# Score products tied to the queue place of the feed-forward products, and a new split of the feed-forward fill, in a fused attention, FFN and MoE kernel

## The chip, the core and the metric

The kernel runs on one core of one Trainium2 chip. The time is device microseconds from the start to the end of one execution. A profile is one execution recorded by the hardware profiler.

## What is computed

Three layers run in one launch. Attention has 4 batches, 8 heads, 576 tokens and 64 channels per head, and each query keeps only the keys whose score reaches its 32nd largest. The second layer is a dense feed-forward network (FFN) from 512 to 2048 and back, with a squared ReLU. The third is a mixture of 8 experts, of which each token uses two.

```python
scores = scale * np.matmul(q, k.transpose(0, 1, 3, 2))
kth = np.partition(scores, -top_k, axis=-1)[..., -top_k:-top_k + 1]
attn = softmax(np.where(scores >= kth, scores, -1e9))
x = attn @ v                                  # 2304 tokens x 512
h = np.maximum(x @ w_in, 0.0)
x = h * h @ w_out
# top 2 of 8 noisy gate logits, then the two experts' outputs, weighted
out[mask] += top2_w[mask, k, None] * (np.maximum(x[mask] @ w1[e], 0.0) @ w2[e])
```

## The kernel before

**Units.** Attention is cut into 80 units. A full unit is two heads of one batch and 128 queries. It has two score tiles of 128 x 576, one per head. A left unit holds the 64 last queries of two heads in one score tile. A unit goes through these steps:

- `scores` (L429) multiplies queries and keys on TensorE (L439: four products for a full unit's tile, eight for a left unit's) into the PSUM tile `ps`. There is one `ps` buffer (L389). ScalarE copies it into the row buffer `sb` (L442, or L444 and L445 for a left unit). A unit has one row buffer, and there are four of them, so a unit takes over the buffer of the unit four before it.
- VectorE searches the 32 largest (L453, L457 and `threshold`, L478). The last steps for one tile are put between the search steps of the next tile.
- `softmax` masks and exponentiates with ScalarE L510, GpSimd L511 and ScalarE L512, one of each per tile.
- TensorE transposes the weights of each tile, four blocks at a time (`transpose4`, L523), and then the last 64 keys and the sums (`rest`, L550 and L551). This last step is the last reader of the row buffer.
- `times_v` (L564) multiplies with V in 20 products. The last of them is noted in `gates`.

**FFN.** When all units of a group of token tiles are done, the FFN of that group, a chunk, is put into a background list. There are seven chunks, of 2, 2, 2, 3, 3, 3 and 3 token tiles. `ffn` (L301) is a generator. Each piece it gives out is one group of three TensorE products: L357 to L359 into PSUM tile `pf` (first matrix) or L320 to L322 into `acc` (second matrix). ScalarE L364, L369, L370 and GpSimd L371 stand between the two. Weights come from HBM on the SP queue (L344, L345), two buffers each. The first two chunks have other forms (`plain`, `divide`).

**Order.** The program is written as one loop over units (L861). In iteration i it puts out, in this order: fills 0 and 1, the first transposition of unit i-1, fill 2, the first score tile of unit i+2, fill 3, the second transposition of unit i-1, fill 4, the second score tile of unit i+2, fill 5, `rest` of unit i-1, fill 6, `times_v` of unit i-1, fill 7. A fill puts out a share of the unit's FFN work, given by the list `FILLS`; what is put out too much or too little is carried over. The unit's FFN work (`rate`) is set so that a chunk's FFN ends about when the next chunk's units do.

The queue order of each engine is not the program's: a planner takes, by its own estimate of times, the ready instruction with the best priority. FFN work has a priority 350 instructions later than its place (`FILL_LATER`, L734), and the copies L442 one that is 300 earlier (`SOON`). `tc.issue_after(x)` keeps instructions behind x in the queue of x's own engine, with no semaphore. All FFN products stand in `with behind()`, which puts them behind the last product of the `times_v` put out last:

```python
def behind():
    return tc.issue_after(gates[-1].ins) if gates else nullcontext()
```

Score products have no such tie before the change. After the 80 units, the FFN of the last chunk and the experts (L640 to L715) run.

Of the kernel before, what the change touches and what calls it, by code (L numbers as in the profile page):

```python
# [17 lines left out]
P = 128  # L18
# [10 lines left out]
IN_PSUM = 14  # L29
LEFT_WEIGHT = 0.6  # L30
FILLS = [0.02, 0.1, 0.15, 0.2, 0.15, 0.1, 0.2, 0.1]
ROUTE_WAIT = 30
LAST_WAIT = 8
EXPERT_WAIT = 60
EARLY = 3
SOON = 300
FILL_LATER = 350
PROMPT = 350
CONVERT_LATER = 200
# [15 lines left out]
def attention_ffn_moe(ctx: ExitStack, tc: tile.TileContext, q, k, v, w_ffn, w_route, noise, w_exp, out,  # L55
# [3 lines left out]
    nc = tc.nc  # L59
# [5 lines left out]
    NF = DFF // P  # L65
    NFE = F // P
    NC = DM // P
    HS = S // 2
    NFULL = S // P
    LEFT = S - NFULL * P  # L70
# [10 lines left out]
    whole = [nc.dram_tensor(f"whole{tag}{f}", (P, 2, DM), F32, kind="Internal").ap() for f in range(NF)]  # L81
# [105 lines left out]
    def route(t0, xrs):  # L187
# [50 lines left out]
        nc.gpsimd.tensor_tensor(mb[:, 0:nt, :], o1, o2, op=ALU.add)  # L238
        yield LAST_WAIT if after else ROUTE_WAIT
        pp = ps_f.tile([P, DM], F32, name="pf")  # L240
# [49 lines left out]

    vpools = []

    gates = []

    def behind():
        return tc.issue_after(gates[-1].ins) if gates else nullcontext()
# [4 lines left out]
    def ffn(t0, nt, xT):  # L301
        n = nt * P
        acc = []
        plain, divide = t0 == 0, t0 == CHUNKS[0]

        def second(f, wo, gt):
            if f == 0:
                while fronts:
                    front()
                acc.extend(ps_acc.tile([P, DM], F32, name="acc") for _ in range(nt))  # L310
            for tt in range(nt):
                sl = slice(tt * P, (tt + 1) * P)
                if plain:
                    with behind():
                        nc.tensor.matmul(acc[tt], gt[:, 0, sl].bitcast(F32), wo[:, 0, :].bitcast(F32),
                                         start=(f == 0), stop=(f == NF - 1))
                    yield True, 0.8
                    continue
                with behind():
                    nc.tensor.matmul(acc[tt], gt[:, 0, sl], wo[:, 0, :], start=(f == 0), stop=False)  # L320
                    nc.tensor.matmul(acc[tt], gt[:, 0, sl], wo[:, 1, :], start=False, stop=False)  # L321
                    nc.tensor.matmul(acc[tt], gt[:, 1, sl], wo[:, 0, :], start=False, stop=(f == NF - 1))  # L322
                yield True, 0.65

        prev = None
        for f in range(NF):
            if after:
                wi, wo = (mpools[0].tile([P, 2, DM], F32R, name=name, bufs=3) for name in ("wif", "wof"))
            else:
                wi, wo = (fpool.tile([P, 2, DM], F32R, name=name, bufs=2) for name in ("wi", "wo"))  # L330
            if plain:
                for i, w in enumerate((wi, wo)):
                    nc.sync.dma_start(w[:, 0, :].bitcast(F32), whole[f][:, i])
            elif divide:
                raw = vpools[0].tile([P, 2 * DM], U32, name="raw", bufs=4 if keep is not None else 2).bitcast(F32)
                nc.sync.dma_start(raw, whole[f].rearrange("p a d -> p (a d)"))
                for i, (w, eng) in enumerate(((wi, nc.gpsimd), (wo, nc.vector))):
                    part = raw[:, i * DM:(i + 1) * DM]
                    with prompt():
                        nc.scalar.activation(w[:, 0, :], part, AF.Copy)  # L340
                        eng.tensor_tensor(w[:, 1, :], part, w[:, 0, :].bitcast(F32), op=ALU.subtract)
                    nc.sync.dma_start(wsc[f][:, i], w.bitcast(F32))
            else:
                nc.sync.dma_start(wi.bitcast(F32), wsc[f][:, 0])  # L344
                nc.sync.dma_start(wo.bitcast(F32), wsc[f][:, 1])  # L345
            ph = after[0].tile([P, DM], F32, name="ph") if after else ps_f.tile([P, DM], F32, name="pf")
            for c in range(NC):
                sl = slice(c * P, (c + 1) * P)
                if plain:
                    with behind():  # L350
                        nc.tensor.matmul(ph[:, 0:n], wi[:, 0, sl].bitcast(F32), xT[:, 0, c, 0:n].bitcast(F32),
                                         start=(c == 0), stop=(c == NC - 1))
                    if c < NC - 1:
                        yield False, 0.2 * nt
                    continue
                with behind():
                    nc.tensor.matmul(ph[:, 0:n], wi[:, 0, sl], xT[:, 0, c, 0:n], start=(c == 0), stop=False)  # L357
                    nc.tensor.matmul(ph[:, 0:n], wi[:, 0, sl], xT[:, 1, c, 0:n], start=False, stop=False)  # L358
                    nc.tensor.matmul(ph[:, 0:n], wi[:, 1, sl], xT[:, 0, c, 0:n], start=False, stop=(c == NC - 1))  # L359
                if c < NC - 1:  # L360
                    yield False, 0.163 * nt
            r = fpool.tile([P, CH], F32, name="r")
            with prompt():
                nc.scalar.activation(r[:, 0:n], ph[:, 0:n], AF.Relu)  # L364
                gt = fpool.tile([P, 2, CH], F32R, name="gt")
                if plain:
                    nc.scalar.activation(gt[:, 0, 0:n].bitcast(F32), r[:, 0:n], AF.Square)
                else:
                    nc.scalar.activation(r[:, 0:n], r[:, 0:n], AF.Square)  # L369
                    nc.scalar.activation(gt[:, 0, 0:n], r[:, 0:n], AF.Copy)  # L370
                    nc.gpsimd.tensor_tensor(gt[:, 1, 0:n], r[:, 0:n], gt[:, 0, 0:n].bitcast(F32), op=ALU.subtract)  # L371
            yield True, 0.163 * nt
            if prev is not None:
                yield from second(*prev)
            prev = (f, wo, gt)
        yield True, 0.65
        yield from second(*prev)
        if t0 + nt == NTT:
            for e in range(EARLY):
                nc.vector.tensor_scalar(base[:, e:e + 1], base[:, e:e + 1], float(e * NT + PARTS[0][1]), None,  # L380
                                        op0=ALU.max)
        routing.append([route(t0, evacuate(acc)), 1])
        if not after:
            fronts.append(t0)
# [44 lines left out]
    def scores(pairs, sb, whole, then):  # L429


        ps = ps_s.tile([P, 2, 512], F32, name="ps")
        for i, (st, kt, par) in enumerate(pairs):
            for n in range(2):
                if whole:
                    at, w = n * HS, HS
                else:
                    at, w = ((LEFT * par, NFULL * P), (0 if par else NFULL * P, LEFT))[n]
                nc.tensor.matmul(ps[:, n, 0:w], st, kt[:, at:at + w], start=(i == 0), stop=(i == len(pairs) - 1))  # L439
        with tc.high_priority(SOON):  # L440
            if whole:
                nc.scalar.activation(sb.rearrange("p (n s) -> p n s", n=2), ps[:, :, 0:HS], AF.Copy)  # L442
# [3 lines left out]
        w = apool.tile([P, S], F32, name="w", bufs=4)  # L446
        if keep is not None:
# [3 lines left out]
            for i in range(SEGS + 1):  # L451
# [3 lines left out]
                if i > 0:  # L455
                    sl, top = parts[i - 1]
# [58 lines left out]
    def recip(sm):  # L515
        with tc.high_priority(SOON):
            nc.scalar.add(sm, sm, EPS)
# [10 lines left out]
    def finish(av, rt, dst, j, off, n, plain):  # L528
        if plain:
            with tc.high_priority(SOON):  # L530
                nc.vector.tensor_tensor(dst[:, 0, j, off:off + n].bitcast(F32), av[:, 0:n], rt, op=ALU.mult)
            return
        x = apool.tile([P, P], F32, name="x", bufs=4)
        with tc.high_priority(SOON):
            if n == P:
# [189 lines left out]
    state = {"safe": True, "due": 0.0, "chunk": 0, "routed": 0}  # L725
# [4 lines left out]
    def step(n):  # L730

        state["due"] += n
        at = tc.cur_priority
        tc.cur_priority = at + FILL_LATER  # L734
        while state["due"] > 0 and (background or routing):
# [125 lines left out]
    for i in range(NU):  # L861
        credit = rate(i)

        def fill(part):
            step(credit * part)

        fill(FILLS[0] + FILLS[1])
        for f, a in todo.get(i, []):
            f(*a)
        q_split(i + AHEAD + 2)  # L870
        if i + AHEAD < NU:
            start(i + AHEAD)
        else:
            flush()
        if i > 0:
            next(gens[i - 1])
        fill(FILLS[2])
        if i + AHEAD < NU:
            next(gens[i + AHEAD])
        fill(FILLS[3])  # L880
        if i > 0:
            next(gens[i - 1])
        fill(FILLS[4])
        if i + AHEAD < NU:
            next(gens[i + AHEAD])
        fill(FILLS[5])
        if i > 0:
            next(gens[i - 1])
        fill(FILLS[6])
        if i > 0:  # L890
            close(i - 1)
        fill(FILLS[7])
        side(convs, CONVERTS, CONVERT_LATER)
        if i >= ZEROS_FROM:
            side(zeros, 1, ZEROS_LATER)
# [232 lines left out]
```

## Time and profile before

| what | before |
|---|---|
| median of 3 runs | 1333.97 us (1333.89 to 1338.11) |
| the profiled execution's own time | 1336.86 us |
| its span, first to last instruction | 1335.1 us |
| PE, matmul busy | 1241.5 us (93%) |
| PEld, weight loads busy | 1071.8 us (80%) |
| DVE / ACT / POOL busy | 899.2 / 856.6 / 746.2 us |
| mean granted TensorE clock | 0.985 of full speed |

PE is TensorE's matmuls, PEld its weight loads, which overlap them. DVE is VectorE, ACT ScalarE, POOL GpSimd, SP the engine whose queue starts most transfers. Matmuls are pipelined, and the duration shown of one is longer than the distance to the next, so a busy PE need not be a PE at its peak. Idle time of an engine matters only where that engine sets the end.

### The profile page before, as it was taken

The numbers are of one execution on the slowest core, as the hardware profiler recorded it, in microseconds if no ns is written. First come the engines' busy times: TensorE is split into PE (matmuls) and PEld (weight loads), VectorE is DVE, ScalarE is ACT, GpSimd is POOL, SyncE is SP. The second block draws the span as 40 slices with busy tenths as digits, with TensorE's granted clock in tenths as the row PEclk, the third lists the DMA queues.
The fourth block names the chain that finished last, engine by engine and source line by source line (L and its number), as shares of the span: only waits on it lengthen the run. The fifth ranks groups of instructions, "written<-read, shape, count | busy, mean of one in ns | idle before, by whom it ended". The sixth has DMA issues, their size and how long they took to land.

```text
span 1335.1 us, 26136 instructions
## 1 busy us (share of the span) xinstructions
PE 1241.5 (93%) x8030; PEld 1071.8 (80%) x8030; DVE 899.2 (67%) x4557; ACT 856.6 (64%) x1886; POOL 746.2 (56%) x1243
## 2 busy tenths in 40 slices
PE   3769889989998999999999999999999999999997
PEld 2556667777887888888888888899899999988886
DVE  8999989998986899978677410255534343444554
ACT  6878879989897889987878653543433333332443
POOL 5857798887786676767655635333432241503221
PEclk9889999999999999999999999999999999999999
DMA  9998886875675554366534689366643443534464
GB/s 333 361 368 292 274 273 235 309 260 181 219 231 193 166 174 157 106 211 204 168 115 158 205 297 332 113 198 197 192 151 117 143 136 119 174 103 143 141 202 140
DMA packets 93302, 270.06 MB, mean 202 GB/s; under 512 B 11612, under 2 KB 11740, under 8 KB 93152
## 3 DMA queue, kind: packets, MB, share of 16 engines
q1 hardware_dynamic: 83872, 239.91, 54.3%
q0 software_dynamic: 9280, 28.40, 5.9%
q8 instruction: 65, 1.06, 0.3%
q14 instruction: 85, 0.70, 0.2%
HBM read 209.90 MB, written 60.45 MB: 202 GB/s over the span
## 4 chain that ended last, share of the span: by engine, by line
PE 61%; ACT 13%; DVE 11%; DMA 7%; issue 5%; POOL 3%; SPq 0%; POOLq 0%; DVEq 0%; ACTq 0%
PE pa L564 5%; PE ph L693 5%; PE ph L695 4%; PE ph L694 4%; PE acc L676 4%; PE acc L674 4%; PE acc L675 4%; PE ps L439 4%; PE pa L523 3%; PE acc L322 3%; PE acc L320 3%; PE acc L321 3%; DMA raww<-in_exp 3%; PE pf L357 2%; PE pf L358 2%
## 5 line engine op out<-in xcount | busy, mean ns | idle before, releaser
L511 POOL TENSOR_TENSOR sb<-sb,w 128x576 f32<-128x576 f32 x144 | 205.8, 1430 | 63.3 <-ACT w L510 59.3
L453 DVE MAX8 m<-sb 128x8 f32<-128x115 f32 (+1 forms) x720 | 190.3, 264 | 53.1 <-ACT sb L442 47.6
L457 DVE MATCH_REPLACE8 w<-m,sb 128x115 f32<-128x115 f32 (+1 forms) x720 | 187.1, 263 | 0.0
L699 ACT ACTIVATE ht<-ph 128x384 fp32r<-128x384 f32 (+1 forms) x128 | 55.8, 436 | 195.2 <-PE ph L695 177.0
L715 POOL DMA_INDIRECT out<-y,info x40 | 45.1, 1127 | 242.4 <-DVE y L714 224.7
L439 PE MATMUL ps<-K,qt 128*128 128x288 f32 (+2 forms) x640 | 131.4, 333 | 43.9 <-ACT sb L442 30.0
L700 DVE SCALAR_TENSOR_TENSOR ht<-ph,ht 128x384 fp32r<-128x384 f32 (+1 forms) x128 | 62.7, 490 | 161.7 <-ACT ht L699 148.5
L693 PE MATMUL ph<-xe,wi 128*128 128x256 f32 (+1 forms) x512 | 159.9, 312 | 1.9 <-ACT wi L686 1.0
L695 PE MATMUL ph<-xe,wi 128*128 128x256 f32 (+1 forms) x512 | 159.2, 311 | 0.2 <-DVE wi L687 0.2
L694 PE MATMUL ph<-xe,wi 128*128 128x256 f32 (+1 forms) x512 | 158.9, 310 | 0.0
L439 PEld LDWEIGHTS ps<-K,qt 128*128 128x128 f32 x640 | 103.7, 204 | 64.4 <-ACT sb L442 37.7
L512 ACT ACTIVATE sb<-sb,keep 128x576 f32<-128x576 f32 x144 | 112.5, 781 | 28.1 <-POOL sb L511 27.6
L674 PE MATMUL acc<-wo,ht 128*128 128x512 f32 x320 | 125.8, 397 | 0.4 <-DVE y L714 0.4
L675 PE MATMUL acc<-wo,ht 128*128 128x512 f32 x320 | 125.3, 395 | 0.0
L510 ACT ACTIVATE w<-sb,keep 128x576 f32<-128x576 f32 x144 | 111.3, 775 | 16.4 <-POOL keep L506 16.2
L371 POOL TENSOR_TENSOR gt<-r,gt 128x384 fp32r<-128x384 f32 (+1 forms) x96 | 90.7, 946 | 53.2 <-ACT gt L370 39.9
L481 DVE MAX8 m<-w 128x8 f32<-128x288 f32 x288 | 116.0, 443 | 0.1
L357 PE MATMUL pf<-xT,wi 128*128 128x384 f32 (+1 forms) x320 | 106.0, 331 | 5.4 <-ACT r L364 3.9
L523 PE MATMUL pa<-ident,sb 128*128 128x128 f32 x576 | 94.8, 289 | 16.5 <-ACT sb L512 7.1
L676 PE MATMUL acc<-wo,ht 128*128 128x512 f32 x320 | 108.9, 401 | 0.0
L525 ACT COPY pt<-pa 128x512 f32<-128x512 f32 x144 | 83.2, 578 | 32.1 <-PE pa L523 21.2
L693 PEld LDWEIGHTS ph<-xe,wi 128*128 128x128 f32 x512 | 96.4, 188 | 8.5 <-ACT wi L686 1.4
(211 smaller groups left out, 3511.9 us busy)
## 6 DMA issues: line engine op xcount, KB each, us to landing
raww<-in_exp SPq DMA_DIRECT2D x88, 512.0 KB
wi<-wsc SPq DMA_DIRECT2D x64, 512.0 KB
wo<-wsc SPq DMA_DIRECT2D x64, 512.0 KB
raw<-in_ffn SPq DMA_DIRECT2D x32, 512.0 KB
xs<-xr SPq DMA_DIRECT2D x40, 258.0 KB
mr<-xs SPq DMA_DIRECT2D x40, 258.0 KB
qn<-in_q SPq DMA_DIRECT2D x40, 256.0 KB
whole<-ca SPq DMA_DIRECT2D x32, 256.0 KB
```

The costliest lines, as they stand in the source:

```text
L357: nc.tensor.matmul(ph[:, 0:n], wi[:, 0, sl], xT[:, 0, c, 0:n], start=(c == 0), stop=False)
L439: nc.tensor.matmul(ps[:, n, 0:w], st, kt[:, at:at + w], start=(i == 0), stop=(i == len(pairs) - 1))
L453: in_turn(nc.vector.max(parts[i][1], sb[:, parts[i][0]]))
L457: in_turn(nc.vector.match_replace(out=w[:, sl], in_to_replace=top, in_values=sb[:, sl], imm_value=NEG))
L511: nc.gpsimd.tensor_tensor(sb, sb, w, op=ALU.subtract)
L523: nc.tensor.transpose(pt[:, c * P:(c + 1) * P], e[:, c * P:(c + 1) * P], ident)
L674: queued(nc.tensor.matmul(acc[t], hs[i][:, 0, sl], wo[:, 0, :], start=(f == 0), stop=False))
L675: queued(nc.tensor.matmul(acc[t], hs[i][:, 0, sl], wo[:, 1, :], start=False, stop=False))
L676: queued(nc.tensor.matmul(acc[t], hs[i][:, 1, sl], wo[:, 0, :], start=False, stop=(f == NFE - 1)))
L693: queued(nc.tensor.matmul(ph[:, 0:n], wi[:, 0, sl], xe[i][:, 0, c, :], start=(c == 0), stop=False))
L694: queued(nc.tensor.matmul(ph[:, 0:n], wi[:, 0, sl], xe[i][:, 1, c, :], start=False, stop=False))
L695: queued(nc.tensor.matmul(ph[:, 0:n], wi[:, 1, sl], xe[i][:, 0, c, :], start=False, stop=(c == NC - 1)))
```

## The change

It keeps the last FFN product that was put out (`ffn_last`). From the time that two FFN chunks are finished (`state["chunk"] >= 2`), the products of a score tile are put behind that product in TensorE's queue. The reference is taken out of the list when it is used, so a tile with no FFN product put out since the last tile has no tie. From the same point on, the shares of the fills come from a second list. `route`, the experts and all tile sizes and buffers stay as they are.

```diff
+FILLS_SPACED = [0.02, 0.13, 0.35, 0.1, 0.15, 0.05, 0.15, 0.05]
 FILLS = [0.02, 0.1, 0.15, 0.2, 0.15, 0.1, 0.2, 0.1]
+SPACED_FROM = 2
...
-    gates = []
+    gates, ffn_last = [], []
...
-                    nc.tensor.matmul(acc[tt], gt[:, 1, sl], wo[:, 0, :], start=False, stop=(f == NF - 1))
+                    third = nc.tensor.matmul(acc[tt], gt[:, 1, sl], wo[:, 0, :], start=False, stop=(f == NF - 1))
+                    ffn_last[:] = [third]
...
-                    nc.tensor.matmul(ph[:, 0:n], wi[:, 1, sl], xT[:, 0, c, 0:n], start=False, stop=(c == NC - 1))
+                    third = nc.tensor.matmul(ph[:, 0:n], wi[:, 1, sl], xT[:, 0, c, 0:n], start=False, stop=(c == NC - 1))
+                    ffn_last[:] = [third]
...
-        for i, (st, kt, par) in enumerate(pairs):
+        between = state["chunk"] >= SPACED_FROM and ffn_last
+        with tc.issue_after(ffn_last.pop().ins) if between else nullcontext():
+            for i, (st, kt, par) in enumerate(pairs):
...
-        fill(FILLS[0] + FILLS[1])
+        fills = FILLS_SPACED if state["chunk"] >= SPACED_FROM else FILLS
+        fill(fills[0] + fills[1])
...
-        fill(FILLS[2])
+        fill(fills[2])
```

The other five fills are edited in the same way.

## Rows read from the trace of the kernel before

**Rows 1.** The page, its first line: the span.
```profile
span 1335.1 us, 26136 instructions
```
**Rows 2.** Windows by stage: PE, PEld, DVE, ACT, POOL busy, granted clock, DMA share, GB/s.
```profile
300.00:550.00 250.00, 235.29 (x1821) 204.39 (x1821) 216.73 (x1466) 216.74 (x512) 188.11 (x298) 0.99 0.56 185
550.00:770.00 220.00, 217.76 (x1566) 190.70 (x1566) 160.84 (x1064) 172.48 (x393) 140.48 (x233) 1.00 0.52 169
860.00:1336.00 476.00, 464.85 (x2632) 417.66 (x2629) 225.38 (x406) 172.42 (x336) 145.38 (x310) 1.00 0.48 151
```
**Rows 3.** Waits of PE from 300 to 770 us: total, times, longest.
```profile
PE ps L439 <- ACT sb L442: 8.7, 10, 1.9
...
PE pf L357 <- DMA wi<-wsc: 1.1, 1, 1.1
```
**Rows 4.** Line L442 from 300 to 770 us: its count, its releaser, its waiters.
```profile
L442 ACT ACTIVATE sb<-ps x77: 623/651/732, 302.6 to 740.2; 128x576 f32<-128x576 f32 x77
...
PE ps L439: 4.3, 7
...
DVE m L453: 45.7, 28
```
**Rows 5.** Timeline of PE around 361 us: start, us, what, idle before.
```profile
359.16 0.69 PE L439 MATMUL ps<-K,qt 128*128 128x288 f32 x4
...
360.82 0.27 PE L551 MATMUL pa<-ident,rb 128*128 128x128 f32 x1
363.00 1.23 PE L439 MATMUL ps<-K,qt 128*128 128x288 f32 x4 [1.91 <-ACT sb L442]
364.16 0.70 PE L564 MATMUL pa<-t,vt 128*64 128x128 f32 x4
```
**Rows 6.** Timeline of ACT in the same stretch.
```profile
362.30 0.65 ACT L442 ACTIVATE sb<-ps 128x576 f32<-128x576 f32 x1
```
**Rows 7.** Window 360 to 366 us, all engines; the eighth figure is the granted clock.
```profile
360.00:366.00 6.00, 4.09 (x30) 3.44 (x30) 6.00 (x44) 4.64 (x13) 5.76 (x9) 0.76 0.82 271
```
**Rows 8.** Timeline of PE from 600 to 605 us.
```profile
600.43 0.27 PE L551 MATMUL pa<-ident,rb 128*128 128x128 f32 x1
...
600.94 0.69 PE L439 MATMUL ps<-K,qt 128*128 128x288 f32 x4
...
601.70 0.39 PE L320 MATMUL acc<-wo,gt 128*128 128x512 f32 x1
601.93 0.40 PE L321 MATMUL acc<-wo,gt 128*128 128x512 f32 x1
...
603.17 0.44 PE L564 MATMUL pa<-t,vt 128*64 128x128 f32 x4
603.44 1.04 PE L564 MATMUL pa<-pt,vt 128*64 128x128 f32 x16
```
**Rows 9.** Groups of PE from 300 to 780 us, shapes apart.
```profile
L320 PE MATMUL acc<-wo,gt 128*128 128x512 f32 x180 | 72.1, 412 | 2.5 <-DMA wo<-wsc 1.1 <-ACT w L510 1.0 <-ACT gt L370 0.4
...
L357 PE MATMUL pf<-xT,wi 128*128 128x384 f32 x192 | 67.1, 349 | 0.5 <-ACT r L364 0.5
...
L564 PE MATMUL pa<-pt,vt 128*64 128x128 f32 x864 | 57.3, 275 | 0.0
...
L357 PE MATMUL pf<-xT,wi 128*128 128x256 f32 x64 | 19.2, 300 | 2.7 <-ACT r L364 1.6 <-DMA wi<-wsc 1.1
```
**Rows 10.** Line L511 alone: POOL busy and count from the start to 400 and to 700 us.
```profile
0.00:400.00 400.00, 106.12 (x74) 0.95 0.81 278
0.00:700.00 700.00, 190.86 (x134) 0.97 0.68 230
```
**Rows 11.** Line L523 alone, the same stretches: PE and PEld busy and count.
```profile
0.00:400.00 400.00, 48.49 (x284) 33.57 (x284) 0.95 0.81 278
0.00:700.00 700.00, 85.98 (x520) 60.15 (x520) 0.97 0.68 230
```

More of the change, by code (lines that the diff above doesn't have):

```diff
@@ L432, in scores @@
         ps = ps_s.tile([P, 2, 512], F32, name="ps")
-        for i, (st, kt, par) in enumerate(pairs):
[L434 to L439, printed above, removed]
+        between = state["chunk"] >= SPACED_FROM and ffn_last
+        with tc.issue_after(ffn_last.pop().ins) if between else nullcontext():
+            for i, (st, kt, par) in enumerate(pairs):
+                for n in range(2):
+                    if whole:
+                        at, w = n * HS, HS
+                    else:
+                        at, w = ((LEFT * par, NFULL * P), (0 if par else NFULL * P, LEFT))[n]
+                    nc.tensor.matmul(ps[:, n, 0:w], st, kt[:, at:at + w], start=(i == 0), stop=(i == len(pairs) - 1))
         with tc.high_priority(SOON):
@@ L876, in attention_ffn_moe @@
             next(gens[i - 1])
-        fill(FILLS[2])
+        fill(fills[2])
         if i + AHEAD < NU:
             next(gens[i + AHEAD])
-        fill(FILLS[3])
+        fill(fills[3])
         if i > 0:
             next(gens[i - 1])
-        fill(FILLS[4])
+        fill(fills[4])
         if i + AHEAD < NU:
             next(gens[i + AHEAD])
-        fill(FILLS[5])
+        fill(fills[5])
         if i > 0:
             next(gens[i - 1])
-        fill(FILLS[6])
+        fill(fills[6])
         if i > 0:
             close(i - 1)
-        fill(FILLS[7])
+        fill(fills[7])
         side(convs, CONVERTS, CONVERT_LATER)
```

## The prediction, made before the changed kernel was run

> **What bounds the kernel now.** I read the windows by stage first [rows 2]. From 860 us on, the experts keep PE busy for 464.85 of 476 us. From 550 to 770 us attention and FFN keep it busy for 217.76 of 220. From 300 to 550 us it is 235.29 of 250. So PE sets the end from the third FFN chunk on, and the visible idle time is 14.7 us in the first of these stretches and 2.2 us in the second. All work that is moved inside 300 to 1336 us stays on PE, so the time can only change by the holes in PE. The change reaches the stretch of about 305 to 770 us, in which the 80 units' second half runs (about 53 units).
>
> Next come the waits of PE [rows 3]. Most of the visible holes are one wait: score products for the copy L442 that empties the only `ps` buffer, 8.7 us in 10 waits, 0.87 us each. The reader is to see that nothing else in this view comes near it; the wait for a weight tile, kept for comparison, is 1.1 us.
>
> Then I looked at one of them in the timeline. At 359.16 a unit's first score tile is multiplied. Its copy starts only at 362.30 [rows 6], after `rest` (L551, 360.82) has released the row buffer of the unit four before. The second score tile waits at the head of the PE queue until 363.00, 1.91 us idle, and only then `times_v` of the old unit runs (364.16) [rows 5]. So the first tile was multiplied 5.0 us before `times_v` of the unit four before, sat in `ps`, and blocked the next tile. At 600 us the order is the same: `rest` 600.43, score tile 600.94, `times_v` 603.17 [rows 8].
>
> Last, the slack behind the search. By 400 us, 74 tiles have begun their subtraction L511 and 284/4 = 71 have begun their transposition; by 700 us it is 134 and 520/4 = 130 [rows 10, 11]. So 3 to 4 tiles lie between, at 300/60 = 5.0 us per tile: 15 to 20 us. The subtraction and the exponential that follow take about 3 us of it by their share of POOL (190.86/134 = 1.4 us for L511 [rows 10]) and an estimate of as much again for the exponential. A tile then waits some 12 to 17 us for PE. PE is not waiting for softmax.
>
> **The change, part by part.**
>
> *The tie.* In iteration i the score tiles of unit i+2 go behind an FFN product which itself stands behind `times_v` of unit i-2, the unit four before. So the order "tile, then `times_v`" that rows 5 and 8 show is turned round. What FFN lies between `times_v` and the first tile is fills 7, 0, 1 and 2: 0.05 + 0.02 + 0.13 + 0.35 = 0.55 of a unit's FFN. Between the first and the second tile it is fills 3 and 4: 0.25. From the second tile to `times_v` it is 0.20. The old list has 0.37, 0.35 and 0.30 at these places, without being binding.
>
> The FFN of a unit: products of 512 columns follow each other in 601.93 - 601.70 = 0.23 us [rows 8]; by columns 384 and 256 make 0.173 and 0.115 (estimates). Three products per piece: 3 x (180 x 0.23 + 192 x 0.173 + 64 x 0.115) = 246 us, over 864/16 = 54 units [rows 9]: 4.6 us per unit. So 0.55 is 2.5 us, 0.25 is 1.15 us, 0.20 is 0.9 us.
>
> *What it removes.* When the first tile comes after `times_v` and 2.5 us more, `rest` has long released the row buffer, and the copy starts when ACT is free. The wait of rows 5 is gone. Upper bound: all 8.7 us [rows 3]. In the same hole the clock fell: from 360 to 366 us the granted clock is 0.76, between the levels of 1.2 and 2.4 GHz [rows 7], after PE had stood still from about 361.1 to 363.0 [rows 5]; that is (1 - 0.76) x 6 = 1.4 us. Together 10.1 us. Lower bound: nothing, if the waits only change their place.
>
> *What it adds.* No semaphore is added; the tie is queue order on PE. But the second tile must not find `ps` full. Between the tiles lie at least 1.15 us of FFN, and the copy takes 0.65 us [rows 4], so ACT may be late by about 0.5 us before PE waits. ACT was idle before only 7 of 77 copies [rows 4], so it is often late. Bounds: no wait at all (0), or 0.87 us, the mean wait of now, at each of some 38 full units (77/2): 33 us. I take 4 waits, 3.5 us: the planner sees most of a full `ps` in advance and puts FFN, transpositions or `rest` in front, all of which are ready there, and the worst cause of late copies, the row buffer, is gone. Behind a waiting tile on PE stand `rest`, `times_v` and FFN; the search waits for the copy.
>
> *What the scores lose.* The first tile of rows 8 would come not at 600.94 but after `times_v` (603.44 + 1.04 = 604.48) and 2.5 us: about 607.0, 6 us later against the rest. VectorE already waits 45.7 us in 28 waits for copies [rows 4], and it will wait more, but it has room: 216.73 busy of 250 and 160.84 of 220 [rows 2]. The 6 us come out of the 12 to 17 us that finished tiles wait. I cost it at nothing; the cover is what is left, 6 to 11 us. If a route step on ACT and POOL eats that, the transposition L523 is late next, and `times_v` and the gated FFN with it. Bound: 0 to some 5 us.
>
> *The new shares.* They sum to 1.00, not 1.02: 0.02 x 4.6 x 53 = 4.9 us of FFN goes behind attention. PE does it there as it would here: in the third row it is busy for 464.85 of 476 us [rows 2], so the price is 0, with bounds of plus and minus 1 us. Pieces put out before the first tile rise from 0.27 to 0.50 of a unit within the iteration, 1.1 us. The SP transfers of `wi` and `wo` and the ACT and POOL steps of these pieces (L364 to L371) move by as much; past the `qn` load of the same iteration on SP and the splitting of keys and queries on POOL that is at most one load. The only wait for `wi` is 1.1 us [rows 3]: bounds plus and minus 1.1 us, taken as 0.
>
> **The sum.** -8.7 - 1.4 + 3.5 = -6.6 us. The profiled execution took 1336.86 us, 1.8 us more than its span [rows 1] and 2.9 more than the median of 1333.97 us, so the same gain makes 1330.3 us of the profile and 1327.4 us of the median. A measurement of this kernel tells about 0.3% (4 us) from no change.
>
> **A page against it.** The ten waits are on one tile with one buffer [rows 3]. If the single buffer were their cause, an order of work would move them and not end them: about 1334 us. The Trainium skill (Perfetto Trace Analysis, Optimization Strategy) says that a gap which repeats on the engine that should be saturated can mean too few buffers in SBUF or PSUM. The trace agrees in that `ps` is the tile waited for. It does not agree that it happens steadily: 10 waits at 77 copies.
>
> **The rivals.**
>
> *Nothing is gained.* The waits remain 10 to 13 in number, at the second tile. For it: one buffer, and ACT is rarely idle. Against: rows 5 and 6 show the copy held by the row buffer, which the order cures. 10.1 us back at 0.87 us is 12 waits. Time 1334 us, give or take 4.
>
> *Slower: the two tiles of a unit stand closer than before.* The words of the change say 0.35 of the FFN between the two tiles. The list does not do that: 0.35 stands ahead of the first tile, and the share between them falls from 0.35 to 0.25, 1.6 to 1.15 us, while 0.75 stands on the other side. If ACT is late by over 0.5 us in two of three full units, that is 25 waits of 0.87 us: +21.8 - 10.1 = +11.7 us, 1346 us. It decides from 12 waits on. For it: only 7 of 77 copies found ACT idle. Against: the copies have priority, and the planner can put other ready work ahead of the tile.
>
> *Much faster: the first stretch gets as dense as the second.* All visible holes of 300 to 550 us are 14.7 us; the weight loads give the same: 204.39/250 = 81.8% against 190.70/220 = 86.7%, and 250 x (1 - 81.8/86.7) = 14.1 us. Time 1320 us. For it: a regular order ends the waits of other products too. Against: only 8.7 us stand before scores. The Trainium skill (Perfetto Trace Analysis, Identifying the Most-Contended Engine) judges the room left on TensorE by the weight loads' share and not by matmul busy time; by that page there is room of some 14 us. The rows agree that the two shares differ, and say nothing on whether this edit gets it.
>
> **How the numbers follow.** Forecast (1322 to 1332): 0.46. Nothing gained: 0.24. Slower (1338 to 1350): 0.22. Much faster: 0.08. Of the forecast, 0.06 lies above 1330 us, within 0.3% of before, and of "nothing gained" 0.03 lies above 1338. Faster: 0.40 + 0.08 = 0.48. Slower: 0.22 + 0.03 = 0.25. The same: 0.06 + 0.21 = 0.27. The range goes from the much faster case less 2 us, 1318, to the price of the slower one, 1346; left out are half of the much faster and half of the slower case, 0.15. The forecast's own range is 1322 to 1332 us.
>
> **What would show it.** In the changed profile a unit's first score tile comes after `times_v` of the unit four before, by about 2.5 us; its copy starts within 1 us; "PE ps L439 <- ACT sb L442" falls from 8.7 to some 3.5 us from 300 to 770 us (line numbers shift by a few); the clock hole at 360 us is gone; the difference of L511 and L523 counts falls from 3 or 4 tiles to about 2; the wait of VectorE for copies rises above 45.7 us at no cost. I am wrong if the score wait grows over 10 us (the slower rival), if transpositions wait for L512 (the slack was not there), or if PE's holes go and the end does not move.

## The result, and the profile after

The changed kernel takes 1353.35 us (median of 5 runs, 1351.08 to 1354.95) against 1334.28 us for the kernel before: ratio 1.0141, 95% interval 1.0121 to 1.0162. It is slower by 19 us; I had forecast 6.6 us faster. The profiled executions differ by 1352.3 - 1335.1 = 17.2 us of span [rows 1]. Line numbers have moved: scores L445, their copy L448, subtraction L517, transpositions L529, `rest` L556 and L557 with its copy L559 and its broadcast `rb` L554, `times_v` L570.

The first line of the page, and the windows by stage in the columns of rows 2, of the changed kernel; the first two answer to the first two of rows 2:

```profile
span 1352.3 us, 26134 instructions
```

```profile
300.00:550.00 250.00, 226.48 (x1751) 197.99 (x1750) 203.41 (x1369) 206.61 (x486) 176.44 (x281) 0.99 0.53 179
550.00:770.00 220.00, 216.19 (x1561) 188.36 (x1559) 169.61 (x1153) 177.69 (x402) 148.86 (x243) 1.00 0.50 169
300.00:400.00 100.00, 85.46 (x696) 72.80 (x695) 79.31 (x517) 81.32 (x197) 72.89 (x119) 0.99 0.59 199
400.00:500.00 100.00, 91.48 (x697) 80.84 (x696) 81.13 (x560) 82.97 (x195) 68.13 (x118) 0.99 0.49 167
770.00:1353.00 583.00, 567.57 (x3211) 506.05 (x3209) 241.43 (x458) 223.76 (x440) 190.47 (x415) 1.00 0.50 168
```

The same windows of the kernel before, which the prediction had not cut so finely:

```profile
300.00:400.00 100.00, 94.44 (x771) 81.30 (x771) 88.26 (x591) 90.25 (x223) 80.28 (x130) 0.98 0.64 209
400.00:500.00 100.00, 93.35 (x694) 81.53 (x694) 82.79 (x564) 80.79 (x186) 69.56 (x119) 1.00 0.53 177
...
770.00:1336.00 566.00, 553.50 (x3131) 495.12 (x3128) 238.77 (x447) 216.07 (x423) 186.10 (x407) 1.00 0.52 170
```

PE's idle time from 300 to 400 us went from 5.6 to 14.5 us: half of the loss lies there, 9.0 of 17.2 us. From 400 to 500 it is 1.9 us more, and over all of 550 to 770 us 1.6 us more (3.8 against 2.2 [rows 2]). In the last stage PE is idle for 14.7 us up to the end of the span (582.3 - 567.57) where it was 11.6 (565.1 - 553.50), 3.1 us more. The 14.1 us that PE is busy longer there are work not done earlier.

The waits of PE from 300 to 790 us (total, times, longest):

```profile
PE pa L570 <- ACT t L559: 14.2, 15, 2.4
PE pa L557 <- POOL rb L554: 3.9, 1, 3.9
PE acc L322 <- ACT gt L374: 2.2, 2, 1.6
PE acc L324 <- POOL gt L375: 2.2, 3, 0.9
...
PE ps L445 <- ACT sb L448: 0.7, 2, 0.5
```

The score products' wait went from 8.7 us [rows 3] to 0.7. In its place `times_v` waits 14.2 us for the ScalarE copy L559 of its own unit's `rest`, and `rest` once 3.9 us for `rb`, the sums spread out by POOL: PE now stands before the last steps of a unit. No transposition L529 waits for its exponential here. Line L517 (POOL) and L529 (PE, four per tile) from the start to 400 and to 700 us, as rows 10 and 11:

```profile
0.00:400.00 400.00, 100.88 (x71) 0.95 0.80 275
...
0.00:400.00 400.00, 46.76 (x274) 32.20 (x275) 0.95 0.80 275
...
0.00:700.00 700.00, 184.30 (x129) 0.97 0.66 228
...
0.00:700.00 700.00, 85.38 (x516) 59.62 (x516) 0.97 0.66 228
```

By 400 us 71 subtractions stand against 274/4 = 68.5 transposed tiles, 2.5 tiles between where it was 3; by 700 us 129 against 129, none, where it was 4. By this count there are no tiles in hand at 700 us, and at 400 us hardly fewer than before; the pairing of tiles further below says how long a finished tile still stood.

The worst hole, on PE:

```profile
391.70 0.19 PE L248 MATMUL pf<-mb,onesb 128*128 128x8 bf16 x2
395.81 0.33 PE L557 MATMUL pa<-ident,rb 128*128 128x128 f32 x1 [3.92 <-POOL rb L554]
397.22 0.69 PE L570 MATMUL pa<-t,vt 128*64 128x128 f32 x4 [1.08 <-ACT t L559]
```

and on POOL and on ScalarE:

```profile
387.49 2.83 POOL L405 TENSOR_TENSOR K<-kn,K 64x576 fp32r<-64x576 f32 x2
390.40 0.20 POOL L512 TENSOR_TENSOR keep<-m,cb 128x4 f32<-128x4 f32 x1
390.67 2.78 POOL L405 TENSOR_TENSOR K<-kn,K 64x576 fp32r<-64x576 f32 x2
393.54 0.45 POOL L548 TENSOR_TENSOR xT<-x,xT 128x128 fp32r<-128x128 f32 x1
393.95 1.39 POOL L517 TENSOR_TENSOR sb<-sb,w 128x576 f32<-128x576 f32 x1
...
395.46 0.29 POOL L554 TENSOR_SCALAR rb<-sm 128x128 f32<-128x128 f32 x1
```

```profile
395.38 0.78 ACT L518 ACTIVATE sb<-sb,keep 128x576 f32<-128x576 f32 x1 [1.79 <-POOL sb L517]
...
396.81 0.35 ACT L559 COPY t<-pa 128x256 f32<-128x256 f32 x1
```

POOL splits four keys of the third batch in 5.6 us and only then comes to the next subtraction and to `rb`, 0.29 us of work. ScalarE does the exponential of another tile (395.38) and then the 0.35 us copy for which `times_v` waits. The kernel before also splits four keys of this batch between 376 and 382 us, and loses 3.2 of the 50 us from 350 in all, where the changed kernel loses 9.4. The two windows, before and after:

```profile
350.00:400.00 50.00, 46.76 (x376) 40.75 (x375) 46.34 (x310) 45.08 (x110) 44.00 (x58) 0.97 0.70 229
```

```profile
350.00:400.00 50.00, 40.64 (x335) 35.63 (x336) 41.77 (x279) 39.41 (x93) 40.72 (x53) 0.97 0.64 220
```

### The profile page after: what moved, and what is told of

It is laid out like the page before. It is cut to its first block, busy times and chain, and to the rows that moved or that the text cites. A ratio compares the mean times of both kernels' runs of the same rounds, so it can differ in the third digit from the quotient of the medians.

```text
span 1352.3 us, 26134 instructions
## 1 busy us (share of the span) xinstructions
PE 1243.8 (92%) x8030; PEld 1072.8 (79%) x8030; DVE 896.8 (66%) x4557; ACT 858.7 (64%) x1886; POOL 746.4 (55%) x1243
## 3 DMA queue, kind: packets, MB, share of 16 engines
q8 instruction: 65, 1.06, 0.3%
## 4 chain that ended last, share of the span: by engine, by line
PE 50%; issue 7%; ACT 4%; DMA 4%; POOL 2%; DVE 1%; POOLq 0%; SPq 0%; DVEq 0%; ACTq 0%
PE ph L699 4%; PE ph L701 4%; PE ph L700 4%; PE acc L682 4%; PE acc L680 3%; PE acc L681 3%; PE pa L570 3%; PE acc L322 3%; PE acc L324 3%; PE acc L323 3%; PE ps L445 2%; PE pf L360 2%; PE pf L362 2%; DMA raww<-in_exp 2%; PE pf L361 2%
## 5 line engine op out<-in xcount | busy, mean ns | idle before, releaser
L517 POOL TENSOR_TENSOR sb<-sb,w 128x576 f32<-128x576 f32 x144 | 205.7, 1430 | 57.2 <-ACT w L516 51.9
L721 POOL DMA_INDIRECT out<-y,info x40 | 44.3, 1106 | 248.1 <-DVE y L720 230.6
L445 PE MATMUL ps<-K,qt 128*128 128x288 f32 (+2 forms) x640 | 127.6, 328 | 35.5 <-ACT sb L448 21.5
L445 PEld LDWEIGHTS ps<-K,qt 128*128 128x128 f32 x640 | 104.0, 202 | 52.9 <-ACT sb L448 27.7
L360 PE MATMUL pf<-xT,wi 128*128 128x384 f32 (+1 forms) x320 | 106.6, 333 | 4.2 <-ACT r L368 2.0
L529 PE MATMUL pa<-ident,sb 128*128 128x128 f32 x576 | 94.8, 288 | 16.9 <-ACT sb L518 7.3
L361 PE MATMUL pf<-xT,wi 128*128 128x384 f32 (+1 forms) x320 | 101.8, 318 | 0.4 <-POOL xT L548 0.4
```

What stands on the lines that cost most here:

```text
L517: nc.gpsimd.tensor_tensor(sb, sb, w, op=ALU.subtract)
```

## The experiments

All were timed in three rounds against the kernel before, on one chip per group (medians of before: 1335.82, 1336.36, 1335.83, 1336.27 and 1337.3 us). Where not said otherwise, the edit is to the changed kernel.

**The two parts by themselves.** The tie with the old shares, and the new shares without the tie:

```
-FILLS_SPACED = [0.02, 0.13, 0.35, 0.1, 0.15, 0.05, 0.15, 0.05]
+FILLS_SPACED = FILLS
```

> The tie of the score products stays, the fills keep the old shares (0.02, 0.1, 0.15, 0.2, 0.15, 0.1, 0.2, 0.1). Theory (the tie is the cause: the score tile no longer lies between rest and times_v, so times_v waits for ScalarE's copy of the rest tile): 1345 to 1355 us, the waits of times_v for that copy 10 to 20 us from 300 us on. Rival (the new shares are the cause): 1331 to 1337 us, as before.

```
-        between = state["chunk"] >= SPACED_FROM and ffn_last
+        between = False
```

> The new shares of the fills from the third chunk on, no tie. Theory (tie): 1331 to 1338 us, the waits of times_v for the copy of the rest tile under 3 us, the waits of score products for the copy L448 still 6 to 10 us. Rival (shares): 1348 to 1355 us.

Tie only: 1340.46 us, ratio 1.0033 (1.0016 to 1.005); `times_v` waits 9.2 us for L559, scores 0.7 us. Shares only: 1343.31 us, 1.0069 (1.0049 to 1.009). Here scores still wait, 7.5 us in 6 waits, so longer at a time, and the granted clock falls behind them. PE's timeline at the longest wait, and windows (the last figure but two is the clock):

```profile
451.96 1.33 PE L445 MATMUL ps<-K,qt 128*128 128x288 f32 x4 [3.14 <-ACT sb L448]
```

```profile
450.00:455.00 5.00, 3.04 (x22) 2.76 (x24) 2.39 (x14) 3.67 (x9) 2.36 (x2) 0.53 0.03 11
455.00:460.00 5.00, 5.00 (x27) 4.50 (x26) 4.26 (x30) 2.45 (x5) 1.82 (x4) 0.79 0.00 2
...
400.00:500.00 100.00, 92.77 (x663) 80.19 (x664) 80.41 (x539) 77.21 (x179) 64.08 (x112) 0.95 0.47 155
```

After PE stood still for 3.14 us the clock is near its lower level of 1.2 GHz. PE worked for only 3.04 of the first 5 us, so an estimate of what that took from its work is (1 - 0.53) x 3.04 + (1 - 0.79) x 5 = 2.5 us. From 400 to 500 us PE is as busy as in the kernel before (92.77 and 93.35 us), but at a mean clock of 0.95 in place of 1.00: at most 5 of the 7.5 us by which this kernel is slower. Both times lie between what the two theories gave, so neither part is free and neither is the cause alone. By the medians the two together cost 19.1 us, more than their sum of 12.1 us (4.6 and 7.5). By the intervals one costs 2 to 7 us, the other 6.5 to 12 and both together 16 to 22, so the excess is only just clear of noise.

**Which of the two tiles.** With the new shares, only the first or only the second tile of a full unit tied (`first` is handed to `scores`: true for a full unit's first tile and for the one tile of a left unit, false for the second; so left units are tied in the first run and free in the other):

```
-        between = state["chunk"] >= SPACED_FROM and ffn_last
+        between = state["chunk"] >= SPACED_FROM and ffn_last and first       # or: not first
```

> The change, but only the first score tile of a unit is tied; the second is free again. Theory (the free tile slips between rest and times_v): 1338 to 1346 us, waits of times_v under 8 us. Rival (the tie of the first tile costs the lead and with it the time): 1350 to 1355 us.

> The change, but only the second score tile of a unit is tied; the first is free and keeps its lead. Theory (the tied second tile is missing between rest and times_v): waits of times_v 8 to 14 us, time 1343 to 1352 us. Rival (the lead of the first tile is what matters): 1338 to 1343 us, no more than the shares alone cost.

First only: 1347.94 us, 1.0076 (1.005 to 1.0103); `times_v` waits 13.3 us, `rest` 3.9, in a profile of the slowest of its four runs (span 1351.7 us; the others took 1345.3 to 1348.8). Second only: 1336.71 us, 0.9999 (0.9987 to 1.0011), `times_v` 5.3 us, scores 2.3, no wait for `rb`. Each pair of expectations missed: the first run lies between its two, the second below both. So the waits before `times_v` come with the tie of the first tile, with which a unit's search begins. What that tie costs in time by itself is not clear: with the new shares it is 7 to 14 us by the interval, and the new shares without a tie are 6.5 to 12. The second tile's tie alone takes back what the new shares cost by themselves (1336.7 against 1343.3 us); added to the first tile's it costs 5.4 us more (1353.35 against 1347.94). With the old shares that second tie is no better:

```
-FILLS_SPACED = [0.02, 0.13, 0.35, 0.1, 0.15, 0.05, 0.15, 0.05]       # tie of the second tile only
+FILLS_SPACED = FILLS
```

> Only the second score tile of a unit is tied, from the third chunk on, with the old shares (that tie with the new shares took 1336.7, no different from the kernel before). If the new shares carry a cost of their own that the tie does not remove (9 us without a tie), this one is faster than the kernel before: 1327 to 1332, with score waits near 2 us and L570's wait for ScalarE near 6. If the cost of the shares was only that of score products going early into a full tile, which the tie removes, the time is 1334 to 1339.

1338.92 us, 1.0029 (1.0016 to 1.0042): the second expectation, and nothing that beats the kernel before.

**The order of the queue itself.** If the loss were a bad order of `rest`, second tile and `times_v`, another order should give it back. `times_v` tied behind the last FFN product too; the second tile put out after `rest`; the copy L559 at the priority of the score copies; and the second tile tied behind `rest` with `times_v` behind the last tile:

```
+        filled = state["chunk"] >= SPACED_FROM and ffn_last
+        with tc.issue_after(ffn_last[-1].ins) if filled else nullcontext():     # e3: around times_v
```

> The change, and times_v is put behind the FFN product put out last as well, so that fill 6 comes between rest and times_v. Theory (the order of rest and times_v costs the time): the waits of times_v fall from 14 us to under 8 us and the time to 1338 to 1347 us. Rival (the lead of the search is lost, whatever stands between rest and times_v): 1350 to 1356 us, the time moves to waits for softmax and the sums.

```
+        late = fills is FILLS_SPACED
-        if i + AHEAD < NU:                    # e4: the second tile's step is moved
+        if not late and i + AHEAD < NU:
...
+        if late and i + AHEAD < NU:
+            next(gens[i + AHEAD])
```

> The change, and from the third chunk on the second score tile is put out after rest and ahead of times_v (before: ahead of rest). Theory (order): a score tile of 0.5 us lies between rest and times_v again, the waits of times_v fall from 14 us to under 6 us, 1335 to 1345 us. Rival (lost lead): 1350 to 1356 us.

```
-        nc.scalar.copy(t5.rearrange("p a s -> p (a s)"), p5[:, 0:2 * P])
+        with tc.high_priority(SOON):
+            nc.scalar.copy(t5.rearrange("p a s -> p (a s)"), p5[:, 0:2 * P])
```

> The change, and the copy of the rest tile (L559) gets the early priority of the score copies on ScalarE; the PE order is left nearly as it is. Theory (times_v stands at the head of PE with nothing between rest and itself, and the copy stands behind other work on ScalarE): waits of times_v 14 us to 5 to 9 us, time 1343 to 1349 us. Rival (the lead of the search is lost, and PE waits somewhere whatever is done): 1351 to 1356 us.

```
+        tie = ffn_last.pop() if between and first else last_rest[-1] if between and last_rest else None
+        with tc.issue_after(tie.ins) if tie else nullcontext():
...
+        with tc.issue_after(score_last[-1].ins) if state["chunk"] >= SPACED_FROM else nullcontext():   # times_v
```

> The change with the second score tile tied behind rest, not behind an FFN product, and times_v tied behind the score tile put out last: the order rest, score tile, times_v is forced in full units. Theory (cover between rest and times_v): waits of times_v under 6 us, those of score products under 4 us, time 1335 to 1345 us. Rival (lost lead): 1350 to 1356 us.

They took 1366.26 (1.0226, 1.0206 to 1.0246), 1354.13 (1.0146, 1.0128 to 1.0163), 1354.37 (1.0133, 1.0104 to 1.0162) and 1354.3 us (1.0132, 1.0108 to 1.0157). The first is worse: `times_v` comes later still, and FFN products wait 11.8 us for the gated parts on POOL. The others change nothing in the time: `times_v` waits 14.6, 14.1 and 11.9 us. But they clear the order less than it seems, since the queue hardly followed the edits. On PE, between the end of `rest` and the first product of `times_v`, a score tile lies in 45 of the last 49 units of the kernel before, and something in all of them. In the changed kernel a score tile lies there in 33 of 49 units, with nothing at all in 6; in the second of these runs 32 and 5, in the fourth 37 and 3. That `times_v` lost work which used to cover its copy stays a rival.

**The sum of the shares.** In the kernel before, without any tie:

```
-FILLS = [0.02, 0.1, 0.15, 0.2, 0.15, 0.1, 0.2, 0.1]
+FILLS = [0.02, 0.1, 0.15, 0.2, 0.15, 0.1, 0.18, 0.1]
```

> The kernel before with one share altered: 0.18 in place of 0.20 behind the third step, so that the shares add up to 1.00 and not 1.02. Two theories of why the new shares without the tie cost 9 us (1343.3 against 1335.8). If the sum does it (FFN work falls behind its credit and piles up at the ends of chunks), this kernel shows most of it: 1339 to 1344, with half-speed clock stretches between 400 and 460 us as there. If the places of the shares do it, and the sum is free as I priced it, 1333 to 1338.

1337.35 us, 1.0017 (1.0004 to 1.003). So the sum costs 0.5 to 4 us, and the places of the shares the rest of the second experiment's 7.5 us.

**Where the loss lies.** The change from the fourth chunk on:

```
-SPACED_FROM = 2
+SPACED_FROM = 3
```

> The change, tie and shares, but from the fourth chunk on in place of the third. Theory: the dear part is one stretch, 350 to 400 us, where the splits of the third batch's keys fill POOL, ScalarE and VectorE while TensorE has no finished tiles in hand any more. The third chunk is the one that is taken out here, and that stretch lies in it: TensorE is busy 46 to 47.5 of these 50 us as in the kernel before (40.6 in the changed one), the wait of L570 for the ScalarE copy falls from 14.2 to 6 to 9 us, and the time is 1338 to 1345. Rival, a loss spread evenly over the units under the tie: a quarter of them is spared, so 1348 to 1350.

1341.94 us, 1.0047 (1.0029 to 1.0065), inside what the first theory gave and far from the 1348 to 1350 of an even loss. Its window and wait:

```profile
300.00:400.00 100.00, 93.07 (x771) 79.86 (x770) 88.24 (x592) 90.13 (x223) 80.33 (x130) 1.00 0.64 210
```

```profile
PE pa L570 <- ACT t L559: 7.3, 8, 2.1
```

PE is idle for 6.9 us of the stretch, not 14.5. From 350 us it is busy for 45.4 of 50 us, a little under the 46 to 47.5 expected. It stands 6.1 us above the kernel before of its group, where the changed kernel stands 19.1 above: two thirds of the loss belong to the third chunk.

**The key splits.** They stood ahead of the late tiles, so I put them out earlier, then further apart:

```
-        for n, at in enumerate(K_AHEAD):
+        for n, at in enumerate([11, 8, 4, 3] if b > 1 else K_AHEAD):     # e17: [9, 6, 4, 1]
```

> The change, with the first two of the four steps that load and split the keys put out four and two units earlier for the third and fourth batch (eight POOL subtractions of 1.43 us stood between 367 and 394 us). Theory (tiles in hand gone, then a burst of splits on full side engines): TensorE's busy time in 350 to 400 us rises from 40.6 to 43.5 or more, the 3.9 us wait of L557 for rb goes, and the time falls to 1344 to 1350. Rival (the splits are not what the tiles stand behind): the stretch stays below 42 and the time is 1352 to 1356.

> The change with the four key steps of the third and fourth batch at nine, six, four and one units in place of seven, six, four and three, so that the last pair comes three units after the third. If the 3.9 us wait of L557 comes from POOL's splits at 387 to 393 us ahead of L517 and L554, it goes, together with the 1.79 us that L518 waits for L517, and the time is 1345 to 1350. If they only stood there while the tiles were late from something ahead of them, another wait takes its place and the time is 1351 to 1355.

1353.91 us (1.015, 1.0128 to 1.0173) and 1352.59 us (1.0118, 1.0093 to 1.0144), with the same 3.9 us wait for `rb`. The times are those of the rivals, but they don't clear the splits: these never moved. Line L405 (L401 before), eight splits, first and last start, in the two, in the changed kernel and in the kernel before:

```profile
L405 POOL TENSOR_TENSOR K<-kn,K x8: 1400/1429/1440, 367.9 to 392.8; 64x576 fp32r<-64x576 f32 x8
```

```profile
L405 POOL TENSOR_TENSOR K<-kn,K x8: 1412/1426/1437, 368.0 to 392.8; 64x576 fp32r<-64x576 f32 x8
```

```profile
L405 POOL TENSOR_TENSOR K<-kn,K x8: 1402/1430/1438, 367.5 to 392.1; 64x576 fp32r<-64x576 f32 x8
```

```profile
L401 POOL TENSOR_TENSOR K<-kn,K x8: 1402/1418/1440, 357.5 to 380.2; 64x576 fp32r<-64x576 f32 x8
```

What holds them isn't their place in the program. The tie makes them 10 to 12 us later, as it does the score products; there are three key buffers, so I take it that a split waits for the last score product of the old keys. That was not shown, nor was any run made without splits on POOL there.

**Tiles in hand, given back.** Scores put out three units ahead in place of two, with a fifth score buffer. The room came first from a key buffer (control: the changed kernel with that buffer gone, and the kernel before with the same edit):

```
-AHEAD = 2
+AHEAD = 3
...
-            kn = apool.tile([P, 2, S], F32, name="kn", bufs=2)[:, 0:len(h), :]
+            kn = apool.tile([P, 2, S], F32, name="kn", bufs=1)[:, 0:len(h), :]
...
-        e = apool.tile([P, 2 * S], F32, name="sb", bufs=4)
+        e = apool.tile([P, 2 * S], F32, name="sb", bufs=5)
...
+    q_split(2)                    # ahead of the loop: the third unit's scores
+    start(2)
+    next(gens[2])
+    next(gens[2])
```

> The change with one buffer less for arriving keys (kn: one in place of two), the control for the next one. Both theories: keys arrive some units before they are needed, so 1351 to 1357, and the wait of L570 for the ScalarE copy near 14 us.

> The change with scores put out three units ahead of times_v in place of two, a fifth score buffer for it, and one key buffer less for the room. Theory (tiles in hand are what is missing): the wait of L570 for ScalarE falls from 14 to below 6 us, L557's 3.9 us for rb goes, TensorE is busy 44.5 or more of the 50 us from 350, and the time falls to 1336 to 1343. Rival (the tie costs by the order that it gives TensorE and the side engines, not by the tiles in hand): waits and time stay within 3 us of the control, 1350 to 1357.

> The kernel before (no tie, old shares) with scores three units ahead, five score buffers and one key buffer. If tiles in hand beyond those of the kernel before buy nothing, because there the waits are those of score products for the copy (8.7 us), the time is 1333 to 1338. If a part of its V waits (6 us) goes too, 1328 to 1333; if the key buffer or the longer start costs, up to 1342.

The single key buffer alone cost 78 us (1431.93 us, 1.0701, 1.0677 to 1.0725): up to 300 us PE is busy 179.2 us in place of 233.5. So the times expected were all missed. The differences can be read: under the tie the third unit ahead gives 1417.68 us (1.0605, 1.0584 to 1.0627), 14.3 us below the control, and without tie and new shares 1414.34 us (1.0581, 1.0562 to 1.06). Tie and new shares cost 3.3 us there. To narrow it down I took the room from the weight conversions' buffers, four to three, and left the keys alone:

```
-        raw = vpool.tile([P, 2 * n], U32, name="raw", bufs=4 if keep is not None else 2)
+        raw = vpool.tile([P, 2 * n], U32, name="raw", bufs=3 if keep is not None else 2)       # and "ca"
```

> The change with scores three units ahead, five score buffers, both key buffers, and one buffer less for the weight conversions' raw words and codes (four to three each). Theory (tiles in hand): the change then costs 0 to 6 us against its control, the same kernel without tie and shares, where it costs 17 to 19 otherwise; L570's wait for ScalarE is below 10 us and L557 does not wait 3.9 us for rb. Rival (order as such): 14 us or more over the control.

> The kernel before with scores three units ahead, five score buffers, both key buffers, and the conversions' buffers at three: the control. If the key buffer alone cost the 78 us, 1328 to 1340; if the third unit scored before the first values arrive holds up the start as well, up to 1350.

With the change 1355.21 us (1.0126, 1.0083 to 1.0169), without it 1349.0 us (1.0088, 1.0064 to 1.0113): 6.2 us between the medians, 8.1 between the spans (1353.7 and 1345.6). The four runs with the change scatter from 1348.69 to 1359.48 us, so by the two intervals the cost lies between nothing and some 12 us. That fits the theory's 0 to 6 us and leaves the rival's 14 just outside. Window 300 to 400 us and the wait for L559 with the change, then the same window without it:

```profile
300.00:400.00 100.00, 93.22 (x756) 81.37 (x757) 85.22 (x545) 86.45 (x211) 80.46 (x127) 0.98 0.69 229
```

```profile
PE pa L570 <- ACT t L559: 6.8, 11, 1.4
```

```profile
300.00:400.00 100.00, 91.95 (x742) 79.08 (x742) 85.42 (x567) 87.44 (x216) 82.37 (x130) 1.00 0.67 224
```

The 9 us of this stretch are gone, the wait for `rb` too, though the eight splits stand at the same time there (368.8 to 391.4 us).

To see how long a finished tile stands, I paired tiles in order over the last 49 units (87 tiles), from the end of a tile's exponential to its first transposition. In the run with the change and three units ahead a tile stands 14.2 us again under the tie, and 22.5 without it. From the kernel before to the changed one it fell from 14.1 to 6.2 us. The tie takes away 8 us in both cases, and is dear where 14 us are all there is.

A short stand alone doesn't cost the time, though. With the tie alone a tile stands 6.6 us and the loss is 4.6 us; with only the second tile tied it stands 7.2 us and nothing is lost. From 350 to 400 us the mean is 3.5 us in the changed kernel, 3.8 and 3.9 in these two, and 11.3 in the kernel before. What goes along with the loss better is the number of tiles that stood under 3 us: 13 in the changed kernel, 9 with the tie alone, 6 with the second tile's, none in the kernel before and none with three units ahead. The units with nothing on PE between `rest` and `times_v` go the same way: 6, 2, 1, none and none. No run separates the two.

No version is faster than the kernel before. Three units ahead without the tie cost 11.7 us (1349.0 us), and whether by the conversions' buffers or by the third unit put out before the loop was not separated; up to 300 us PE is busy for 231.2 us there and for 234.9 in the kernel before.

## Why the prediction was wrong

**What bounds it.** Right: PE sets the end, and its holes are most of the difference. PE's busy time over the page went from 1241.5 to 1243.8 us, so 14.9 of the 17.2 us are holes.

**What the tie removes.** Right, and more than forecast: the score wait fell by 8.0 us (8.7 to 0.7), where I expected 3.5 to remain, and the copy starts within 1 us of its tile in 68 of 77 cases, where it was 39. One reading under it was not shown: that the row buffer held the copy of rows 6. ScalarE had no gap there; these ran between the end of `rest` (361.09) and the copy (362.30):

```profile
360.90 0.37 ACT L364 ACTIVATE r<-pf 128x256 f32<-128x256 f32 x1
361.16 0.58 ACT L525 COPY pt<-pa 128x512 f32<-128x512 f32 x1
361.62 0.79 ACT L510 ACTIVATE w<-sb,keep 128x576 f32<-128x576 f32 x1
```

The slower rival, the second tile before a full `ps`, did not happen, and neither did the much faster one. The Trainium skill (Perfetto Trace Analysis, Optimization Strategy) says that a repeating gap can mean too few buffers. Here another order of work, with the one `ps` buffer kept, all but ended these waits, and PE's holes grew elsewhere; a second `ps` buffer was not tried.

**What the scores lose: this step failed.** It read "I cost it at nothing; the cover is what is left, 6 to 11 us", with a bound of "0 to some 5 us". The cover itself was well read. By the pairing above a finished tile stood some 14 us, inside the 12 to 17 us of the prediction. Two things in it were wrong.

First the size. I had the first tile come 6 us later, from the one pair of rows 8. Over the last 49 units its distance from its own `times_v` fell from 41.3 to 30.5 us, 11 us and not 6. More than half of that error lies on the side of the kernel before. In rows 8 the tile starts 2.2 us ahead of `times_v` of the unit four before; over those units the mean is 5.5 us (rows 5: 5.0). On the side after, I had it start 3.8 us behind the start of `times_v` (2.5 us behind its end); the mean is 6.2 us and half of the units lie within 5.2. In seven units, all after 570 us, it is over 10 us, as here, where FFN products of more than a unit lie between:

```profile
593.18 0.44 PE L570 MATMUL pa<-t,vt 128*64 128x128 f32 x4
...
603.68 0.70 PE L445 MATMUL ps<-K,qt 128*128 128x288 f32 x4
```

So the shares of a unit's FFN alone don't say where the tied product stands in PE's queue.

Second, an average was taken for a cover. A mean of 6 us left doesn't hide a stretch where POOL is taken for 5.6 us by key splits and ScalarE works off other tiles, and rows 2, over 250 us, do not show that stretch. From 350 to 400 us VectorE, ScalarE and POOL were busy for 46.34, 45.08 and 44.00 of 50 us in the kernel before. Had I cut the windows there, I would have seen three side engines nearly full at once. The sentence "If a route step on ACT and POOL eats that, the transposition L523 is late next, and `times_v` and the gated FFN with it" named two of the three waiters, but by way of a late transposition, which did not come. I gave it a bound of 5 us and no chance of its own. PE waited 14.2 us before `times_v`, 3.9 before `rest` and 4.4 before products that need the gated parts. That the cover was spent is shown by the shorter stand and, within its noise, by the run with three units ahead; why it costs 19 us here and nothing in the run with only the second tile tied is not shown.

**The new shares.** Priced at 0 with bounds of about 1 us, they cost 7.5 us without the tie; the lower clock, in part behind one hole of 3.1 us before a full `ps`, has at most 5 us of it. With the tie that hole is gone. The sum's price of 0 was nearly right (0.5 to 4 us); the places have the rest.

**The clock.** The gain of 1.4 us did not come about. The drop at 360 us is gone, but the granted clock is 0.83 from 395 to 405 us, behind the hole shown above, and 0.83 again from 495 to 505 us. The kernel before has one such drop, 0.83 from 360 to 370 us.

**What would show it.** The list held in part: scores no longer wait, the first tile comes after `times_v` of the unit four before, by 3.9 us from its end at the median, and the difference of the two counts fell to 2.5 and to 0, where I said 2. VectorE's wait for copies, which I expected to rise, stayed (44.3 us in 26 waits against 45.7 in 28). None of my three signs of being wrong names what came: no transposition L529 waits for the exponential in PE's waits, `rest` and `times_v` wait.

**What stays open.** With a unit more in hand the change still costs 3 us by one pair of runs and 6 by the other, which reaches from nothing to 12, and from the fourth chunk on 6 us. Which part of that is the tie's order, the shares or the 3.1 us of more idle time in the last stage was not separated. Nor was it shown how much of the 9 us at 300 to 400 us belongs to the key splits, and how much to work that no longer lies between `rest` and `times_v`.

## What to carry to other kernels

An edit that starts a producer later spends the time that finished work waits in hand, and that is a reserve, not slack. Look at the shortest of these waits, not at their mean over a stage: here means of 6 to 7 us went with losses from nothing to 19 us. Look in short windows for where the side engines are full together, and count what stands ahead of the next tile on each queue there. When an order is tied to "what was put out last", read in the queue where that instruction stands, and over many units: one pair gave 6 us here where the mean was 11. And after an experiment that changes the order of a program, count in the trace whether the queue followed.

## What the runs showed beyond that

One key buffer in place of two cost 78 us in a kernel that loads keys only at batch ends: PE lost 54 us up to 300 us, before the change applies at all. A hole of 3.14 us on PE, up to 451.96 us, came with granted clocks of 0.53 and 0.79 in the windows of 5 us from 450 us on, so with the 2.5 us estimated above it cost nearly twice its length. And putting key splits out up to four units earlier left them within a microsecond of where they were: their place in the program did not decide when they ran.
